# Linear attention and a PReLU feed-forward on one core: block 2's attention in rows with one column tile, and batches 0 and 1 used as loaded

## The chip, the cores and the metric

The kernel runs on one core of a Trainium2 chip. The metric is device time in microseconds. The core's engines each run their own queue of instructions: TensorE (PE in the profile; PEld are its weight loads), VectorE (DVE), ScalarE (ACT), GpSimd (POOL) and SyncE (SP). Here POOL issues the loads, SP issues the DMA transposes and some of the stores. Matmuls write PSUM banks, from which VectorE and ScalarE read.

## The reference

```python
def _attn_ref(q, k, v, g_norm):                       # 8 batches, 8 heads, S = 576, D = 64
    kv = np.einsum('bhsd,bhse->bhde', k, v)
    out = np.einsum('bhsd,bhde->bhse', q, kv)
    rms = np.sqrt(np.mean(out * out, axis=-1, keepdims=True) + 1e-06)
    return out / rms * g_norm
def _moe_ref(x, w_in, w_out, alpha):                  # 4608 tokens, 512 -> 2048 -> 512
    h = x @ w_in
    g = np.maximum(h, 0.0) + alpha * np.minimum(h, 0.0)
    return g @ w_out
x = attn_out.transpose(0, 2, 1, 3).reshape(4608, 512)
```

Inputs and output are float32. The kernel computes in 16 bits and accumulates in 32.

## The kernel before

**Blocks and units.** The 4608 tokens are cut into nine blocks of 512 (w = 0 to 8). A batch has 576 tokens, so a block's four tiles of 128 tokens come from one or two batches. For each block the 2048 hidden columns are made in 16 units of 128: four 128x512 matmuls into one PSUM bank (L507, `m1_mm`), ScalarE's negative part (L514) and VectorE's sum of the two (L518), which gives `gt`, the PReLU in 16 bits. VectorE's and ScalarE's reads free the bank; from block 2 on there are two such banks (h1, h2).

**The second product.** Block 0's is done plainly (L539, 64 matmuls of 512 columns). For blocks 1 to 8 it is done by seven products of half size, in Strassen's manner: sums of `gt` on VectorE (L623 to L629, `s_sum`), sums of the weights (`w_sum`), 112 matmuls of 256 columns per block (L688, `prod_mm`), and reads of the finished products into the four quarters of the output (`y_read`, which reads p1, u2, c11, u3, c22, c21, c12). The products of block w − 1 are laid into the units of block w, seven to a unit, in the order 1, 6, 2, 7, 5, 4, 3, into two banks that change places.

**Attention.** The attention of block w + 1 is also laid into the units of block w (`attention`), in one of two forms. A pair is two neighbouring heads.
- Column form (blocks 0, 1, 2): q is transposed on TensorE (L327, `transposes`), k^T v is made for a pair at a time (L371, `step_kv`) and masked to its two 64x64 diagonal squares by VectorE (L379); the output stands with head dimensions on the partitions (L393, `step_ot`), ScalarE squares it (L400), a matmul with a mask of ones sums the squares over the partitions (L416, `ssq_mm`), ScalarE takes the reciprocal root (L420), VectorE multiplies it and g in (L429, `norm`) and writes `xt`.
- Row form (blocks 3 to 8, `W_ROW = 3`): q is transposed by DMA on SP (`dma_t`); k^T v is made per head in 64x64 matmuls, one head of the pair to the left, one to the right half of the columns (L1001, `row_kv`; ScalarE copies them, L1007); the output stands with tokens on the partitions (L452, `rows_mm`, 64x64 matmuls); ScalarE squares 128x512 (L463, `rows_sq`), VectorE sums 64 at a time (L469, `rows_ssq`), ScalarE takes the root (L479), VectorE multiplies (L487, `rows_norm`), and a DMA transpose on SP brings the tile into `xt` (L492).

**Copies.** Batches are loaded by POOL into stages. Batch 0's q and k are regrouped by VectorE for heads side by side (L217, `regroup0`); batch 1's and batch 2's in large copies (`regroup`); from batch 3 on q is loaded ready for the DMA transpose, and ScalarE copies k pair by pair (L195, `regroup_pair`). g is multiplied into w_in by ScalarE during block 2 (`scale_w_in`), so that the norm of later blocks leaves it out.

**Order.** The order on PE, ACT, DVE, POOL and SP is that in which the code issues instructions; tables give the unit of each step (`ATT_1`, `ATT_AT`, `ROW_AT`, `S_AT`, `S_ROW`, `Y_READS`). Before the first unit, block 0's attention is worked out with TensorE kept warm by dummy matmuls (L295), and 64 matmuls of block 0's second product share its units with batch 1's attention.

Of the kernel before, what the change touches and what calls it, by code (L numbers as in the profile page):

```python
# [17 lines left out]
def kernel(  # L18
# [11 lines left out]
    nc = tc.nc  # L30
# [20 lines left out]
    W_ROW = 3  # L51
# [81 lines left out]

    alpha_row = ysb_p.tile([P, D_MODEL], FP32, name="y_sb")
# [11 lines left out]
    for i in range(NBUF):  # L146
        t = {}
        for nm in ("k", "v", "q") if i < 2 else ("k", "v"):
            n = 1 if nm == "v" else T0 if i == 0 else NT
            t[nm] = qkv_p.tile([P, n, H, D], FP16, name=f"{nm}sb{i}")  # L150
            if i > 0 or nm == "v":
                nc.vector.memset(t[nm][REM:P, n - 1, :, :], 0.0)
        bufs.append(t)
    stages = {}

    def load0(nm, j, n=1):
        i, h = divmod(2 * j, HH)
        if (0, nm, i) not in stages:
            stages[0, nm, i] = stage_p.tile([P, HH, T0, D], FP16, name=f"{nm}st", tag=f"{nm}st")
# [5 lines left out]
    def load_main(b, nm, h0=0, h1=H):  # L165
        if (b, nm) not in stages:
            stages[b, nm] = stage_p.tile([P, H, TPP, D], FP16, name=f"{nm}st", tag=f"{nm}st")
# [5 lines left out]
    def load_q(b):  # L173
        st = stage_p.tile([P, TPP, H, D], FP16, name="qst", tag="qst")
# [7 lines left out]
    def buf_of(b, nm):  # L182
        return bufs[min(b, B_NAT) % 2 if nm == "q" else b % NBUF][nm]

    def load_rem(b, nm):
        nc.gpsimd.dma_start(
            out=buf_of(b, nm)[0:REM, 0 if nm == "v" else TPP, :, :],
            in_=srcs[nm][b, :, MAIN:S, :].rearrange("h s d -> s h d"),
        )
# [13 lines left out]

    def load_gated(b):
        load_rem(b, "q")
        if b == B_NAT:
            load_q(b)
        load_rem(b, "k")
        load_main(b, "k")
        if b > B_NAT:  # L210
            load_q(b)
        load_rem(b, "v")
        load_main(b, "v")

    def regroup0(nm, j, n=1):
        i, h = divmod(2 * j, HH)
        nc.vector.tensor_copy(  # L217
            out=bufs[0][nm][0:P0, :, 2 * j : 2 * (j + n), :].rearrange("p t h d -> p h t d"),
            in_=stages[0, nm, i][0:P0, h : h + 2 * n],
        )  # L220

    def regroup_pair(b, nm, j):
        regroup(b, nm, 2 * j, 2 * j + 2, nc.scalar)

# [17 lines left out]
    def scale_w_in(g):  # L242
        i = max(n for n, f0 in enumerate(IN_CUTS[:-1]) if f0 <= g * P)
        f0 = g * P - IN_CUTS[i]
        blk = w_in_sb[i][:, :, f0 : f0 + P]
        nc.scalar.activation(out=blk, in_=blk, func=AF.Copy, scale=g2col[:])

    def load_w_out(i):
        t = w_p.tile([P, GW, D_MODEL], FP16, name=f"w_out_sb{i}")
        for r in range(0, GW, GW // 2):  # L250
            g = i * GW + r
            nc.gpsimd.dma_start(
                out=t[:, r : r + GW // 2, :],
                in_=moe_w_out[g * P : (g + GW // 2) * P, :].rearrange("(g p) m -> p g m", p=P),
            )
        w_out_sb.append(t)
# [20 lines left out]
    for i in range(len(IN_CUTS) - 1):  # L277
        load_w_in(i)
    load_batch(1, ("k",))
    load_w_out(0)  # L280
    load_main(1, "q")
    load_w_out(1)
# [3 lines left out]
    load_w_out(2)  # L286
    load_w_out(3)
    load_rem(1, "q")

# [13 lines left out]
    kv_masked = [const_p.tile([P, NPAIR, P], FP16, name=f"kv_masked{i}") for i in range(2)]  # L303
# [19 lines left out]

    def transposes(qt_ps, c, b, j, ts):
        n = rows(b)
        for t in ts:
# [29 lines left out]
    def dma_t(b, ts=tuple(range(NT))):  # L356
        qt = qt_sb[b % 2][:, :, PAD : PAD + S]
        for t in ts:
            c0, c1 = t * P, min((t + 1) * P, S)
            src = stages[b, "q"][:, t] if t < TPP else buf_of(b, "q")[0:REM, TPP]  # L360
# [5 lines left out]

    def step_kv(b, j, pool=(ps_s, "s")):
        ks, vs = pair_cols(b, "k", j), pair_cols(b, "v", j)
        kv_ps = pool[0].tile([P, P], FP32, name="kv_ps", tag=pool[1])
        for t in range(n_runs(b)):  # L370
            nc.tensor.matmul(  # L371
                out=kv_ps[:],
                lhsT=ks(t),
                rhs=vs(t),
                start=(t == 0),
                stop=(t == n_runs(b) - 1),
            )
        kvs[b, j] = kv_masked[b % 2][:, j, :]
        nc.vector.tensor_mul(out=kvs[b, j], in0=kv_ps[:], in1=mask32[:])  # L379

# [3 lines left out]
    def step_ot(w, j, pool=None, parts=1):  # L384
# [13 lines left out]
        sq = attn_p.tile([P, W], FP16, name="sq_sb")  # L398
# [27 lines left out]
    def norm(w, j, parts=1):  # L426
        ot_ps, rstd = ots.pop((w, j))
        for c in col_parts(parts):
            nc.vector.scalar_tensor_tensor(  # L429
# [9 lines left out]
    def rows_mm(w, i0):  # L439
        o_ps = row_tile([2, 2, NPAIR, D], "or_ps")  # L440
        for i in (i0 + 1, i0):
            b, r = divmod(w * W + i * P, S)
            for j in range(NPAIR):
# [5 lines left out]
                for n, (bb, c) in enumerate(steps):  # L449
                    for h in range(2):  # L450
                        part = slice(h * D, (h + 1) * D)
                        nc.tensor.matmul(  # L452
                            out=o_ps[:, h, i - i0, j, :],
# [4 lines left out]
            ots[w, "r", i] = o_ps[:, :, i - i0]  # L458

    def rows_sq(w, i):  # L460
        o_ps = ots.pop((w, "r", i))
        sq = attn_p.tile([P, 2, NPAIR, D], FP16, name="sq_sb")
        nc.scalar.activation(out=sq[:], in_=o_ps, func=AF.Square)  # L463
        ots[w, "r", i] = (o_ps, sq)

    def rows_ssq(w, i):
        o_ps, sq = ots.pop((w, "r", i))
        ssq = attn_p.tile([P, 2, NPAIR], FP32, name="ssq_r")
        nc.vector.tensor_reduce(  # L469
            out=ssq[:].rearrange("p h j -> p (h j)"),  # L470
            in_=sq[:].rearrange("p h j d -> p (h j) d"),
            axis=mybir.AxisListType.X, op=ALU.add,
        )
        ots[w, "r", i] = (o_ps, ssq)

    def rows_rs(w, i):
        o_ps, ssq = ots.pop((w, "r", i))
        rstd = attn_p.tile([P, 2, NPAIR], FP32, name="rstd_r")
# [5 lines left out]
    def rows_norm(w, i):  # L484
        o_ps, rstd = ots.pop((w, "r", i))
        xr = attn_p.tile([P, NPAIR, 2, D], FP16, name="x_rows", tag="rstd" if i % 2 else "x_rows")
# [9 lines left out]
    gts = {}  # L496
# [15 lines left out]
    def m1_evac(h_ps, w, g):  # L512
        m_sb = gt_p.tile([P, W], FP32, name="m_sb", bufs=2)
        nc.scalar.activation(out=m_sb[:], in_=h_ps[:], func=AF.Relu, scale=-1.0)  # L514
        i, r = divmod(g, 2)
        if (w, i) not in gts:
            gts[w, i] = gt_p.tile([P, 2, W], FP16, name="gt", tag=f"gt{i}")
        nc.vector.scalar_tensor_tensor(  # L518
            out=gts[w, i][:, r, :], in0=m_sb[:], scalar=beta_sb[:, g : g + 1], in1=h_ps[:],
            op0=ALU.mult, op1=ALU.add,  # L520
        )

# [14 lines left out]

    def y_mm(y, w, a, g):
        nc.tensor.matmul(  # L539
            out=y[:], lhsT=gt_cols(w, g, a * P, (a + 1) * P), rhs=w_out_blk(g),  # L540
            start=(g == 0), stop=(g == NF - 1),
# [3 lines left out]
    store_turn = [0]  # L545

# [28 lines left out]
    def y_out(y, w, a):  # L575
        y_sb = ysb_p.tile([P, D_MODEL], FP32, name="y_sb")
        nc.scalar.copy(out=y_sb[:], in_=y[:])
        store_rows(w * W + a * P, y_sb[:], 0, D_MODEL)
# [37 lines left out]
    def s_sum(w, n, k):  # L616
        lo, hi = gts[w, k], gts[w, k + KQ]
        a11, a21 = lo[:, :, 0:HW], lo[:, :, HW:W]
        a12, a22 = hi[:, :, 0:HW], hi[:, :, HW:W]
        t = sum_p.tile([P, 2, HW], FP16, name=f"s{n}", tag=f"s{n}{k}", bufs=2 if n < 3 else 1)  # L620
# [13 lines left out]
    def y_bank(w, n, a):  # L634
        pool, tag = ((ps_y, "y"), (ps_h, "h0"))[(w + (n != "Y")) % 2]
# [108 lines left out]
    Y_ORDER = (1, 6, 2, 7, 5, 4, 3)  # L744
    Y_LIST = [(n, i) for n in Y_ORDER for i in range(2 * NK)]
    PER = len(Y_LIST) // NF
    Y_READS = {2: ("p1",), 5: ("u2",), 7: ("c11",), 9: ("u3",), 11: ("c22",), 14: ("c21",)}
    R_ROW = {2: ("p1",), 5: ("u2",), 7: ("c11",), 14: ("c21",)}
    R_FIRST = {10: "u3", 12: "c22"}
    G_ORDER = [0, 1, 8, 9, 2, 3, 10, 11, 4, 5, 12, 13, 6, 7, 14, 15]  # L750


# [36 lines left out]
    regroup0("q", 1)  # L789
    keep_warm(1)  # L790
    step_t(0, 1, h_at(1))
    regroup0("k", 1)
# [5 lines left out]
    regroup0("q", 2, 2)  # L798
    keep_warm(1)
    step_t(0, 2, h_at(0))  # L800
    regroup0("k", 2)
# [6 lines left out]
    regroup0("k", 3)  # L808
# [358 lines left out]
```

## Time and profile before

| what | value |
|---|---|
| time, median of three runs | 274.64 us (274.28 to 275.09) |
| profiled execution, its own time | 275.59 us |
| its span, first to last instruction | 273.6 us |
| mean granted TensorE clock | 0.994 |
| first unit of block 0 / of block 1 / last matmul's end | 16.05 / 48.09 / 270.27 us |
| DMA | 34.56 MB, mean 126 GB/s |

The span is what the profiler recorded; 2.0 us of the execution's time lie around it. On the page, busy shares are averages over the whole span; the forty slices are 6.8 us each. In a group's line the first figures are an engine's busy time and the mean duration of one; matmuls are pipelined, so that a duration is longer than the distance from one start to the next. What stands in brackets behind an instruction is how long its engine was idle before it, and what released it.

### The profile page before, as it was taken

How to read it: one execution, taken by the hardware profiler on the slowest of the kernel's cores; microseconds unless marked ns; L12 is line 12 of the kernel's file. 1: busy time of each engine (PE TensorE's matmuls, PEld its weight loads, DVE VectorE, ACT ScalarE, POOL GpSimd, SP SyncE). 2: the span in 40 equal slices, each digit the busy share in tenths (PEclk: the TensorE clock that was granted, in tenths of full speed). 3: DMA queues.
4: the chain of work that ended last, by engine and by line, in shares of the span. 5: the costliest groups of instructions: out<-in, count | busy, mean ns of one | idle time of the engine just before them, and what ended most of it. 6: DMA issues, size and time to landing. Idle time of an engine off the chain costs nothing.

```text
span 273.6 us, 5687 instructions
## 1 busy us (share of the span) xinstructions
PE 266.3 (97%) x2181; PEld 170.8 (62%) x2181; DVE 227.9 (83%) x432; ACT 155.9 (57%) x294; POOL 86.2 (32%) x123
## 2 busy tenths in 40 slices
PE   7799999999999999999999999999999999999995
PEld 2364464555666766666666666666666666666794
DVE  6459938899889979997999799979998999877863
ACT  3267555879989865645565556555544553443210
POOL 8773462780733355226421551100110012000200
PEclk9799999999999999999999999999999999999999
DMA  8999999999999689966996699720222122201223
GB/s 161 196 200 199 197 202 189 220 112 162 137 164 180 99 129 149 170 153 113 155 167 147 112 156 164 151 89 19 77 60 77 22 77 60 77 1 41 77 79 116
DMA packets 87343, 34.56 MB, mean 126 GB/s; under 512 B 58884, under 2 KB 85652, under 8 KB 87316
## 3 DMA queue, kind: packets, MB, share of 16 engines
q0 software_dynamic: 58064, 24.35, 69.5%
q1 hardware_dynamic: 28212, 8.83, 17.1%
q10 hardware_dynamic: 1040, 1.02, 1.2%
q8 instruction: 17, 0.28, 0.4%
q14 instruction: 10, 0.08, 0.1%
HBM read 36.71 MB, written 9.44 MB: 169 GB/s over the span
## 4 chain that ended last, share of the span: by engine, by line
PE 95%; DMA 2%; DVE 1%; issue 0%; ACT 0%; POOLq 0%
PE h_ps L507 43%; PE yY L688 15%; PE yX L688 10%; PE yZ L688 10%; PE y L539 5%; DMA vst<-in_v_dram 2%; PE h_ps L530 2%; PE kv_ps L371 2%; PE or_ps L452 1%; PE kv_ps L1001 1%; PE ssq_ps L416 1%; PE qt_ps L327 1%; PE ot_ps L393 1%; PE yZ L683 1%; PE warm_ps L295 0%
## 5 line engine op out<-in xcount | busy, mean ns | idle before, releaser
L507 PE MATMUL h_ps<-xt,w_in_sb 128*128 128x512 f16 x544 | 136.9, 379 | 0.0
L514 ACT ACTIVATE m_sb<-h_ps 128x512 f32<-128x512 f32 x144 | 86.1, 599 | 78.1 <-PE h_ps L507 67.7
L518 DVE SCALAR_TENSOR_TENSOR gt<-m_sb,beta_sb,h_ps 128x512 f16<-128x512 f32 x144 | 106.2, 744 | 24.1 <-ACT m_sb L514 22.5
L507 PEld LDWEIGHTS <-w_in_sb 128*128 128x128 f16 x544 | 52.1, 98 | 40.0
L550 POOL DMA_DIRECT2D out_dram<-y_sb x36 | 22.6, 630 | 134.3 <-ACT y_sb L726 53.4
L688 PEld LDWEIGHTS <-s 128*128 128x128 f16 x496 | 48.5, 98 | 19.1
L688 PEld LDWEIGHTS <-gt 128*128 128x128 f16 x384 | 37.3, 98 | 14.0
L688 PE MATMUL yY<-wsum,s 128*128 128x256 f16 x256 | 36.3, 273 | 0.0
L688 PE MATMUL yX<-w_out_sb,gt 128*128 128x256 f16 x256 | 36.1, 273 | 0.0
L177 POOL DMA_DIRECT2D qst<-in_q_dram x20 | 17.7, 923 | 1.8 <-DMA vst<-in_v_dram 1.8
L688 PE MATMUL yY<-wsum,gt 128*128 128x256 f16 x128 | 17.6, 273 | 0.0
L688 PE MATMUL yZ<-wsum,s 128*128 128x256 f16 x120 | 16.7, 273 | 0.0
L688 PE MATMUL yZ<-w_out_sb,s 128*128 128x256 f16 x120 | 16.7, 273 | 0.0
L487 DVE TENSOR_TENSOR x_rows<-or_ps,rstd_r 128x512 f16<-128x512 f32 x24 | 16.4, 683 | 0.0
L469 DVE TENSOR_REDUCE ssq_r<-sq_sb 128x8 f32<-128x512 f16 x24 | 16.3, 678 | 0.0
L463 ACT ACTIVATE sq_sb<-or_ps 128x512 f16<-128x512 f32 x24 | 14.4, 599 | 2.6 <-PE or_ps L452 2.6
L539 PE MATMUL y<-w_out_sb,gt 128*128 128x512 f16 x64 | 15.8, 379 | 0.0
L625 DVE TENSOR_TENSOR s<-s,gt 128x512 f16<-128x512 f16 x32 | 13.5, 421 | 0.5
L623 DVE TENSOR_TENSOR s<-gt 128x512 f16<-128x512 f16 x32 | 13.4, 418 | 0.0
L629 DVE TENSOR_TENSOR s<-gt,s 128x512 f16<-128x512 f16 x32 | 13.2, 417 | 0.0
L627 DVE TENSOR_TENSOR s<-gt 128x512 f16<-128x512 f16 x32 | 13.0, 418 | 0.0
L720 DVE TENSOR_TENSOR u<-yY,p 128x512 f32<-128x512 f32 x16 | 10.9, 683 | 1.9 <-PE yY L688 1.7
(88 smaller groups left out, 249.9 us busy)
## 6 DMA issues: line engine op xcount, KB each, us to landing
out_dram<-y_sb POOLq DMA_DIRECT2D x16, 256.0 KB, 2.7
kst<-in_k_dram POOLq DMA_DIRECT2D x7, 512.0 KB, 7.9
vst<-in_v_dram POOLq DMA_DIRECT2D x6, 512.0 KB, 10.5
qst<-in_q_dram POOLq DMA_DIRECT2D x20, 128.0 KB, 8.0
w_out_sb<-in_moe_w_out_dram POOLq DMA_DIRECT2D x8, 256.0 KB, 11.7
out_dram<-y_sb SPq DMA_DIRECT2D x5, 256.0 KB, 2.2
w_in_sb<-in_moe_w_in_dram POOLq DMA_DIRECT2D x2, 512.0 KB, 10.0
qst<-in_q_dram POOLq DMA_DIRECT2D x2, 512.0 KB, 12.1
```

The lines of the kernel that those rows point to most:

```text
L177: nc.gpsimd.dma_start(out=st[:, t, :, :], in_=srcs["q"][b, :, t * P : (t + 1) * P, :].rearrange("h p d -> p h d"),)
L463: nc.scalar.activation(out=sq[:], in_=o_ps, func=AF.Square)
L469: nc.vector.tensor_reduce(out=ssq[:].rearrange("p h j -> p (h j)"), in_=sq[:].rearrange("p h j d -> p (h j) d"), axis=mybir.AxisListType.X ...
L487: nc.vector.tensor_tensor(out=xr[:].rearrange("p j h d -> p h j d"), in0=o_ps, in1=rstd[:].unsqueeze(3).to_broadcast([P, 2, NPAIR, D]), op ...
L507: nc.tensor.matmul(out=h_ps[:], lhsT=w_in_blk(c, g), rhs=xts[w][:, c, :], start=(c == 0), stop=(c == NC - 1),)
L514: nc.scalar.activation(out=m_sb[:], in_=h_ps[:], func=AF.Relu, scale=-1.0)
L518: nc.vector.scalar_tensor_tensor(out=gts[w, i][:, r, :], in0=m_sb[:], scalar=beta_sb[:, g : g + 1], in1=h_ps[:], op0=ALU.mult, op1=ALU.add,)
L539: nc.tensor.matmul(out=y[:], lhsT=gt_cols(w, g, a * P, (a + 1) * P), rhs=w_out_blk(g), start=(g == 0), stop=(g == NF - 1),)
L550: engs[store_turn[0] % len(engs)].dma_start(out=dst, in_=src)
L623: nc.vector.tensor_add(out=t[:], in0=a21, in1=a22)
L625: nc.vector.tensor_sub(out=t[:], in0=sums[w, 1, k][:], in1=a11)
L688: nc.tensor.matmul(out=bank, lhsT=lhs, rhs=rhs, start=fresh, stop=(c == NK - 1), skip_group_check=True,)
```

## The change

What the changed kernel does otherwise:

1. `W_ROW` is 2: block 2 takes the row form, except its tile 3, which is done in columns with all four pairs in one bank (`cols_mm`, `cols_sq`, `cols_rs`, `cols_norm`). Batch 2's q is transposed by DMA.
2. Batches 0 and 1 are read from their stages as loaded. Their key-value products are done per head, one head in each half of the columns, and their q transposes too. `regroup0`, `regroup(1, ...)` and `regroup_pair` go; the row form's key-value products read k and v of later batches from the stages (`head_rows`).
3. In the row form the square and its sum over 64 are one ScalarE instruction per head and tile, with an accumulator, unless the table's `red` is 1 for that tile (block 2's three row tiles, one tile of blocks 4 to 7, two of block 8), where they stay one square of 128x512 and a VectorE reduce.
4. w_in is scaled by g during block 0 and the first four units of block 1, mostly on VectorE; from block 1 on the norm leaves g out.
5. Products 1 and 2 of block w are laid into block w's own units and the first two of the next block (`x_prods`, bank y); the other five of block w − 1 go into the units of block w in the order 6, 7, 4, 5, 3 (`yz_prods`, bank h0). Where a read of a product falls in a unit, the unit's `gt` is made after it. The units go in plain order 0 to 15, and the sums have new tables.
6. Loads are issued in another order, those of batches from 3 on unit by unit, some behind a one-element POOL copy of a `gt` (`gate`); three stores of block 0 move to SP in block 2.

```diff
-    W_ROW = 3
+    W_ROW = 2
+    def head_rows(b, nm, h, t):
+        if t < TPP:
+            return stages[b, nm][:, h, t, :]
+        return rem_of(b, nm)[:, h, :]
     def transposes(qt_ps, c, b, j, ts):
+            for i in range(2):
+                src = cols0("q", j, i, t) if b == 0 else head_rows(b, "q", 2 * j + i, t)
+                nc.tensor.matmul(
+                    out=qt_ps[i * D : (i + 1) * D, c : c + n], lhsT=src,
+                    rhs=ident16[0:n, 0:n], is_transpose=True, start=True, stop=True,
...
     def step_kv(b, j, pool=(ps_s, "s")):
+        kv_ps = pool[0].tile([P, D], FP32, name="kv_ps", tag=pool[1])
+        for t in range(NT):
+            for i in range(2):
+                nc.tensor.matmul(
+                    out=kv_ps[i * D : (i + 1) * D, :], lhsT=head_rows(b, "k", 2 * j + i, t),
+                    rhs=head_rows(b, "v", 2 * j + i, t), start=(t == 0), stop=(t == NT - 1),
...
+    def cols_mm(w, i):
+        t = row_tile([2, NPAIR, P], "oc_ps")
+        for j in range(NPAIR):
+            nc.tensor.matmul(
+                out=t[:, 0, j, :], lhsT=kvs[b, j], rhs=qts[b, j][:, r : r + P],
...
     def rows_sq(w, i, half):
+        if ROW_AT[w]["red"][i]:
+            if half == 0:
+                nc.scalar.activation(out=sq[:], in_=o_ps, func=AF.Square)
+            else:
+                nc.vector.tensor_reduce(...)
+            return
+        for j in range(NPAIR):
+            nc.scalar.activation(
+                out=sq[:, half, j], in_=o_ps[:, half, j], func=AF.Square,
+                accum_out=ssq[:, half, j : j + 1],
+            )
...
-    regroup0("k", 3)
...
+    X_LIST, YZ_LIST = products(1, 2), products(6, 7, 4, 5, 3)
+    X_AT = [0, 0, 1, 3, 1, 0, 2, 3, 2, 3, 1, 0, 3, 0, 2, 7, 1, 3]
+    YZ_AT = [3, 6, 7, 5, 5, 6, 7, 3, 6, 8, 4, 4, 6, 5, 5, 0]
...
+    ROW_AT = {2: {'kv': 5, 'mm': {0: ((0,),), 7: ((1, 2), (3,))}, 'sq': (1, 1, 7, 7, 7, 8, 8, 9),
+        'rs': (3, 8, 9, 12), 'norm': (5, 9, 11, 13), 'red': (1, 1, 1, 1)}, 3: {'kv': 2, 'mm': {4:
+        ((1, 0), (3, 2))}, 'sq': (4, 4, 5, 6, 8, 8, 7, 9), 'rs': (6, 7, 9, 11), 'norm': (6, 7, 10,
+        11), 'red': (0, 0, 0, 0)}, 8: {'kv': 99, 'mm': {1: ((1, 0), (3, 2))}, 'sq': (1, 1, 3, 4, 6,
+        6, 9, 9), 'rs': (5, 5, 8, 12), 'norm': (6, 7, 9, 12), 'red': (0, 0, 1, 1)}}
+    for w in range(4, B):
+        ROW_AT[w] = {'kv': 3, 'mm': {4: ((1, 0), (3, 2))}, 'sq': (5, 5, 4, 6, 7, 7, 7, 8), 'rs': (6,
+            7, 8, 11), 'norm': (6, 9, 8, 11), 'red': (0, 0, 1, 0)}
+    COL_TILES = ((2, 3),)
...
+            behind = w > 1 and bool(yz_reads(w - 1, u))
...
+                m1_mm(h_ps, w, u, range(NC))
+                m1_neg(h_ps, w, u)
+                if not behind:
+                    m1_sum(h_ps, w, u)
...
+            x_prods(w, u)
+            if w > 1:
+                yz_prods(w - 1, u)
+            if behind:
+                m1_sum(h_ps, w, u)
```

## The prediction

> **What bounds the kernel now.** I read the page from the top: busy shares, the forty slices, the chain of work that ended last.
>
> ```profile
> PE 266.3 (97%) x2181; PEld 170.8 (62%) x2181; DVE 227.9 (83%) x432; ACT 155.9 (57%) x294; POOL 86.2 (32%) x123
> ...
> PE   7799999999999999999999999999999999999995
> ...
> PE 95%; DMA 2%; DVE 1%; issue 0%; ACT 0%; POOLq 0%
> ```
>
> TensorE is full in all slices but the first two and the last, and it is 95% of the chain. So two things move the end: instructions that leave or join TensorE's stream, and waits. To price the stream I read TensorE's timeline in a stretch that holds the row form, by starts and not by durations (matmuls overlap):
>
> ```profile
> 70.01 1.03 PE L507 MATMUL h_ps<-xt,w_in_sb 128*128 128x512 f16 x4
> ...
> 71.73 0.32 PE L1001 MATMUL kv_ps<-vst,ksb 128*64 128x64 f16 x8
> 71.88 0.20 PE L1001 MATMUL kv_ps<-vsb,ksb 128*64 128x64 f16 x2
> ...
> 72.36 0.20 PE L1001 MATMUL kv_ps<-vsb,ksb 128*64 128x64 f16 x2
> 72.49 1.04 PE L507 MATMUL h_ps<-xt,w_in_sb 128*128 128x512 f16 x4
> 73.36 0.93 PE L688 MATMUL yY<-wsum,s 128*128 128x256 f16 x7
> 74.22 0.76 PE L452 MATMUL or_ps<-kv_masked,qt_sb 64*128 64x64 f16 x40
> ```
>
> Four 128x512 matmuls and seven of 256 columns fill 72.49 to 74.22; over the trace start to start is 0.216 us for 512 columns, 0.163 for 384, 0.109 for 256, 0.056 for 128 and 0.043 for 96. Forty 64x64 key-value matmuls take 71.73 to 72.49, 0.76 us: two column halves start together, so they cost 16 ns each and about 0.1 us at the change of form on either side. The attention matmuls in rows (L452) cost 17.5 ns each with those changes, 14.9 without.
>
> The other place is the start, before the first unit of the first product (16.05 us):
>
> ```profile
> 15.09 0.35 DVE L217 COPY ksb<-kst 96x768 f16<-96x768 f16 x1
> 15.35 0.74 DVE L429 SCALAR_TENSOR_TENSOR xt<-ot_ps,g2col,rstd 128x512 f16<-128x512 f32 x1
> 15.49 0.51 PE L371 MATMUL kv_ps<-vst,ksb 96*128 96x128 f16 x6 [0.30 <-DVE ksb L217]
> 16.05 0.60 PE L815 MATMUL h_ps<-xt,w_in_sb 128*128 128x256 f16 x4
> ```
>
> Here TensorE waits for VectorE's regroup copies. Last, the two evacuating engines, in a steady window (columns: PE, weight loads, DVE, ACT, POOL, clock, DMA share, GB/s) and by shape:
>
> ```profile
> 130.00:160.00 30.00, 30.00 (x270) 20.08 (x269) 27.16 (x50) 17.75 (x36) 12.88 (x18) 1.00 1.15 146
> ```
> ```profile
> L463 ACT ACTIVATE sq_sb<-or_ps 128x512 f16<-128x512 f32 x24 | 14.4, 599 | 2.6 <-PE or_ps L452 2.6
> L469 DVE TENSOR_REDUCE ssq_r<-sq_sb 128x8 f32<-128x512 f16 x24 | 16.3, 678 | 0.0
> L1007 ACT CAST kv_masked<-kv_ps 64x256 f16<-64x256 f32 x10 | 3.7, 368 | 2.0 <-PE kv_ps L1001 2.0
> ```
> ```profile
> 16.97 0.66 ACT L400 ACTIVATE sq_sb<-ot_ps 128x256 f16<-128x256 f32 x2
> ```
>
> TensorE is never idle there, VectorE is busy 27.2 of 30 us, ScalarE 17.8.
>
> **The sum's base.** All durations are of one execution: 275.59 us, of which 273.6 is the span and 2.0 lies around it. It is 0.95 above the median of the runs, 274.64; I subtract the savings from the median.
>
> **TensorE's stream after the start.**
> (a) Batch 2's 20 transposes of 128 columns become DMA transposes: 20 × 0.056 = −1.12.
> (b) Batch 2's 20 key-value pair matmuls (1.12) become 40 halves with their change of form (0.76 + 0.1 = 0.85): −0.27.
> (c) Block 2's attention: four of 128 plus four of 384 columns (0.87) and four sums of squares of 512 (0.86) leave, 1.74; for three tiles come 24 matmuls × 14.9 ns (0.36) with two changes of form (0.38), and for the column tile four of 128 and one of 512 (0.44): 1.18. −0.56.
> (d) Batch 1's 20 pair matmuls (1.12) become 40 halves at 16 ns (0.64), in three groups with 0.19 of changes each (0.57): +0.09.
> (e) Batch 1's 16 full transposes (0.90) become 32 of 64 columns wide. If halves run side by side, as the key-value halves do, they add only two changes, +0.38. If not, 16 × 0.056 = 0.90 on top. The nearest row is the 40 halves in 0.76 us: I take +0.38.
> Block 0's halves lie in the start, below. All other matmuls keep number and shape: moving the products to other units moves nothing in the sum. Sum −1.48 (−0.58 if (e) goes badly).
>
> A rule that speaks against (b), (d) and (e): the Trainium skill, page "TensorEngine Tiling (Array Packing)", Restrictions, says that column tiling disables the fast weight load. In the trace the weight loads of the halves are 112 ns against 98 for full ones, yet 40 matmuls with them fit into 0.76 us, so they are hidden behind each other; were (e)'s loads laid end to end they would be 32 × 112 ns = 3.6 us in place of 0.9 and the total +2.7 worse. The trace speaks against that for key-value halves and does not show transposes.
>
> **The start.** Of the copies of L217, five leave VectorE (0.35 to 0.79 each), and keys, values and q of block 0 go to TensorE as loaded. The last copy held TensorE 0.30 (line above) and the two before it held earlier transposes and key-value groups; between them they sit on the chain to 16.05, behind values that land at about 8.0 us and cannot come earlier. Upper bound of the gain: 1.0, lower 0 if ScalarE's rstd (0.69, ended 15.14) and the norm (0.74) set the end anyway. I take −0.75, since the queue that this norm stood in loses two copies. The chunks then pair 96x96 transposes in 64-column halves: 48 instead of 24, side by side.
>
> **VectorE and ScalarE.** VectorE loses 15 reduces (678 ns), four of the regroup copies of 2048 columns (0.68 to 0.78), five of L217 and four masks; it gains eight scalings of w_in (about 0.7 each, laid in block 0 and block 1's first units, where it has 6.14 of 8 us busy). It ends lighter by some 11 us (16.7 less, 5.6 more), which costs nothing and gains nothing while TensorE is full. ScalarE loses 18 copies of k (611 ns) and 15 squares of 599, and gains 144 squares of 128x64 with a row sum in the accumulator. No row shows an accumulator. From the squares of 256 columns (two in 0.66 us, 0.28 start to start; 0.83 ns per column): 64 columns without accumulator start every 0.12 us. If the accumulator is written as by one more small instruction (the 128x8 row, 298 less 100 of overlap), 0.32. I take 0.22, midway, as neither row is nearer; the cover is TensorE's own stretch. In units 4 to 8 of a steady block TensorE needs five units of 0.864, 35 products of 0.109 and the 24 attention matmuls with changes (0.79): 8.9 us. ScalarE needs five negations (0.49 start to start), one big square and three rstd (0.2): 3.56 + 24x. That equals TensorE's at x = 0.22, and two h banks and four row tiles lend about 0.9: nothing is lost below x = 0.26.
>
> The Trainium skill, "ScalarE: Activation LUTs", section "What ACT_TABLE_LOAD costs", gives 186 ns plus 0.833 per column, with about 93 overlapped: an estimate of 0.146 for 64 columns against 0.12 from the rows, which would leave 0.11 instead of 0.14 for the accumulator and does not change the sign.
>
> **What the moved queues cost.** In block 1, batch 2 now needs its values at unit 5 (about 54.1) for the row key-value products; they landed at 53.7 and POOL's issues before it change (the same loads in another order; six stores that held POOL 3.1 us behind it go to SP later). Its q chunks are transposed on SP from unit 0 on (landing 2.4 to 5.8 after issue, 48.8 and later) and are needed at unit 7 (57.4): 57.2 at the latest. Both are met by under 0.4 us, and what waits is TensorE itself, with all of block 1 behind: I charge +0.5 (0 to +2). The delayed sums of units 2, 5, 8, 11, 14 stand behind a read of a product bank (0.76 + 0.3 + 0.68 + 0.74 = 2.48 against the 2.39 that two banks allow), and eleven gates on POOL hold loads behind a gt: +0.3 (0 to +1). The tail's order changes but its last products and final additions do not: 0.
>
> Total: −1.48 − 0.75 + 0.5 + 0.3 = −1.43, so 273.2.
>
> **Rivals.**
> 1. The accumulating squares are dear (slower). Above 0.26 us each, the four squares of a half stand before the next unit's negation, the h bank comes free late, and TensorE waits in units 4 to 8: 24 × (x − 0.26) in each of blocks 3 to 6, 32 in block 2's units. At x = 0.32 that is some 8 us: 281; at 0.40, 18 us. The row 298 ns for a tiny ScalarE instruction speaks for it, its 0.28 pair spacing for 256 columns against. Chance 0.20.
> 2. Batch 2 comes late (slower). With values or the last chunk 2 to 4 us behind 54.1 and 57.4, TensorE stops in block 1 for as long: 275.3 to 277.5. It decides once transposes land 0.4 later than now; the 0.2 of slack speaks for it, the stores moved out of its way against. Chance 0.13.
> 3. The halves of the transposes don't pair, or the start is bound by rstd and norm as before: (e) costs +0.9, or the start gives 0. 274.0 to 275.2, no change; chance 0.13. Were the weight loads of all 32 transposes laid end to end as well (32 × 112 ns, 2.7 more than taken), 275.9, slower: 0.02, as the forty halves in 0.76 us speak against it. The Trainium skill's rule on column tiling, cited at (e), would come to that.
> 4. As forecast, 271.6 to 273.8: chance 0.52.
>
> **How the numbers follow.** The time is that of case 4, 273.2. A measurement of this kernel tells about 0.3%, 0.82 us, from no change, so faster begins below 273.8. Faster: case 4, 0.52. Same: case 3 and the mild end of 2, 0.15. Slower: rest, 0.33. The range runs from 271.6 (full start gain, no waits) to 279, which leaves out the upper half of case 1 and a little at the bottom; case 4's own range is 271.6 to 273.8.
>
> **What would show it.** Right: TensorE's start to start unchanged per form; qt_ps transposes in halves paired a few ns apart; first 256-column L815 matmul near 15.3; steady ScalarE squares of 128x64 starting every 0.22 or less; block 1 with no wait of TensorE for vst or qt_sb. Wrong: TensorE idle in blocks 2 to 6 behind a negation that stands behind squares; kv_ps waiting for a DMA near 54; block time above the present 27.6.

## The result, and the profile after

The change makes the kernel slower by 0.6%: the ratio to the kernel before is 1.0058, 95% interval 1.0035 to 1.0081, about 276.0 us where the kernel before takes 274.45 (median of 21 runs, 274.09 to 275.62). The ratio leaves out nine of the changed kernel's 21 runs (274.25 to 282.62 us, median 277.74), those from 278.82 on, eight of which had a mean granted clock of 0.994 or 0.988, as one of 129 runs of the kernel before had in the later comparisons, so 0.6% is the low end of what the change costs. 273.2 was forecast. The profiled execution took 276.86 us, its span is 274.7.

The page of the changed kernel, busy shares, slices of TensorE and its clock, and the chain that ended last:

```profile
PE 265.0 (96%) x2286; PEld 168.0 (61%) x2286; DVE 216.9 (79%) x413; ACT 156.3 (57%) x532; POOL 86.0 (31%) x130
...
PE   7999999999999979999999999999999999999995
...
PEclk9999999999999999999999999999999999999999
...
PE 69%; DMA 19%; ACT 4%; DVE 3%; issue 2%; POOL 1%; DVEq 0%; POOLq 0%; ACTq 0%
```

TensorE was 95% of the chain and is 69% now; transfers went from 2% to 19%. TensorE's busy time fell from 266.3 to 265.0, and yet the span grew. TensorE's waits name the places (what waited, for what: us in all, times, longest):

```profile
PE h_ps L631 <- DMA xt<-x_rows: 2.4, 3, 1.8
...
PE y L643 <- DMA w_out_sb<-in_moe_w_out_dram: 0.6, 2, 0.4
PE oc_ps L512 <- DMA qt_sb<-qsb: 0.6, 1, 0.6
PE kv_ps L418 <- DVE kv_masked L393: 0.5, 1, 0.5
PE kv_ps L1122 <- DMA vst<-in_v_dram: 0.4, 1, 0.4
```

Those of the list that lie behind the first unit wait for a transfer, all but one (`kv_masked`, for VectorE). To split the difference I added up TensorE's start-to-start times, from the first matmul of the first unit on, and counted as a gap whatever a matmul took over 0.14 us longer than its columns need:

| us | before | after |
|---|---|---|
| start to the first unit's first matmul | 16.05 | 13.34 |
| from there to the last matmul's end | 254.21 | 258.34 |
| of it gaps | 0.6 | 6.3 |
| of it the stream | 253.6 | 252.0 |
| last matmul's end to the end of the span | 3.3 | 3.0 |

The stream is 1.6 us shorter, where 1.48 was forecast. Four of the gaps of after hold a change of form of about 0.1 us besides the wait, which the table counts as gap, so the stream's own saving is nearer 1.2. The gaps are 5.7 us longer (4.6 in a second profile of the same kernel), where 0.8 was forecast. The start is 2.7 us shorter, but most of that is not the change's: in the profile of before TensorE's granted clock was 0.5 for 3.4 us of the start (the 7 in its second slice), in this one it was not, and the first of batch 0's values, issued at 1.3 us in both, landed at 8.0 us before and at 6.5 after.

The largest wait is that of block 3's first unit for the last of its four row tiles. TensorE's timeline of after, with POOL's and then SP's beside it:

```profile
97.20 0.49 PE L796 MATMUL yY<-wsum,s 128*128 128x256 f16 x3
99.46 0.38 PE L631 MATMUL h_ps<-xt,w_in_sb 128*128 128x128 f16 x4 [1.77 <-DMA xt<-x_rows]
```
```profile
92.43 0.70 POOL L198 DMA_DIRECT2D vsb<-in_v_dram  x1
93.12 0.92 POOL L176 DMA_DIRECT2D vst<-in_v_dram  x1
```
```profile
92.11 1.20 SPq L585 DMA_TRANSPOSE xt<-x_rows  x1
93.40 1.78 SPq L380 DMA_TRANSPOSE qt_sb<-qsb  x1
```

The tile's transpose is issued at 92.11, beside a load of 512 KB of values that the gate now lets go in unit 11. It took 7.3 us to land. In the kernel before, the transpose in the same place was issued at 91.90 and landed in 2.5; there the values had been loaded from 76.57 on. The two landings, after (with the transpose issued at 90.3, which took 3.7) and before:

```profile
DMA to landing us min/median/max: 3.7/5.5/7.3
```
```profile
DMA to landing us min/median/max: 2.5/2.5/2.5
```

### The profile page after: what moved, and what is told of

The parts are those of the page before. It is cut to its first block, busy times and chain, and to the rows that moved or that the text cites. A ratio compares the mean times of both kernels' runs of the same rounds, so it can differ in the third digit from the quotient of the medians.

```text
span 274.7 us, 6154 instructions
## 1 busy us (share of the span) xinstructions
PE 265.0 (96%) x2286; PEld 168.0 (61%) x2286; DVE 216.9 (79%) x413; ACT 156.3 (57%) x532; POOL 86.0 (31%) x130
## 4 chain that ended last, share of the span: by engine, by line
PE 69%; DMA 19%; ACT 4%; DVE 3%; issue 2%; POOL 1%; DVEq 0%; POOLq 0%; ACTq 0%
PE h_ps L600 30%; PE yY L796 14%; PE yZ L796 8%; PE yX L796 8%; DMA w_out_sb<-in_moe_w_out_dram 5%; DMA xt<-x_rows 4%; PE y L643 4%; DMA w_in_sb<-in_moe_w_in_dram 3%; DMA vst<-in_v_dram 3%; ACT sq_sb L562 3%; DMA qst<-in_q_dram 2%; DMA qt_sb<-qsb 2%; PE h_ps L631 2%; PE kv_ps L1122 1%; PE or_ps L499 1%
## 5 line engine op out<-in xcount | busy, mean ns | idle before, releaser
L609 ACT ACTIVATE m_sb<-h_ps 128x512 f32<-128x512 f32 x144 | 88.3, 614 | 81.5 <-PE h_ps L600 59.0
L600 PEld LDWEIGHTS <-w_in_sb 128*128 128x128 f16 x540 | 51.3, 98 | 39.6 <-DMA w_in_sb<-in_moe_w_in_dram 0.4
L655 POOL DMA_DIRECT2D out_dram<-y_sb x32 | 20.5, 646 | 140.4 <-DVE y_sb L838 62.4
L796 PE MATMUL yX<-w_out_sb,gt 128*128 128x256 f16 x256 | 43.1, 273 | 0.0
L796 PE MATMUL yY<-wsum,s 128*128 128x256 f16 x256 | 35.2, 273 | 0.0
L562 ACT ACTIVATE sq_sb<-or_ps 128x64 f16<-128x64 f32 x144 | 31.7, 285 | 2.6 <-PE or_ps L499 2.6
L562 ACT ACTIVATION_READ_ACCUMULATOR sq_sb<-or_ps 128x1 f32 x144 | 31.2, 272 | 0.0
L580 DVE TENSOR_TENSOR x_rows<-or_ps,rstd_r 128x512 f16<-128x512 f32 x27 | 18.5, 687 | 0.9 <-ACT rstd_r L572 0.3
L731 DVE TENSOR_TENSOR s<-gt 128x512 f16<-128x512 f16 x32 | 12.9, 421 | 0.2
L735 DVE TENSOR_TENSOR s<-gt 128x512 f16<-128x512 f16 x32 | 12.4, 419 | 0.0
```

What stands on the lines that cost most here:

```text
L562: nc.scalar.activation(out=sq[:, half, j], in_=o_ps[:, half, j], func=AF.Square, accum_out=ssq[:, half, j : j + 1],)
L580: nc.vector.tensor_tensor(out=xr[:].rearrange("p j h d -> p h j d"), in0=o_ps, in1=rstd[:].unsqueeze(3).to_broadcast([P, 2, NPAIR, D]), op ...
L600: nc.tensor.matmul(out=h_ps[:], lhsT=w_in_blk(c, g), rhs=xts[w][:, c, :], start=(c == 0), stop=(c == NC - 1),)
L609: nc.scalar.activation(out=neg[w, g][:], in_=h_ps[:], func=AF.Relu, scale=-1.0)
L655: engs[store_turn[0] % len(engs)].dma_start(out=dst, in_=src)
L731: nc.vector.tensor_add(out=t[:], in0=a21, in1=a22)
```

## Experiments

Times are ratios to the kernel before on the same chip, with 95% intervals. Theory A: TensorE waits for transfers that land late because others share the DMA engines. Theory B: ScalarE's squares with accumulator, or the engines' own order, hold things up.

**The changed kernel again.** No edit.

> The changed kernel once more, as the yardstick on this chip and for its second profile. Theory A (TensorE waits for transfers that land late): the waits for vst, qt_sb, x_rows and w_out_sb come back at the same four places, with other sizes, since landings vary: 3 to 6 us of waits between 25 and 100 us, time 275 to 278. Theory B (ScalarE's squares with accumulator hold things up): the same waits with the same sizes, within 0.2 us, since engines' durations do not vary.

Measured 1.0091 (1.0074 to 1.0107). The waits came back in the same places, but for that for w_out_sb, which is too short for the list here, and with other sizes:

```profile
PE h_ps L631 <- DMA xt<-x_rows: 1.5, 3, 1.1
...
PE kv_ps L1122 <- DMA vst<-in_v_dram: 0.9, 1, 0.9
PE kv_ps L403 <- DMA vst<-in_v_dram: 0.7, 2, 0.4
PE oc_ps L512 <- DMA qt_sb<-qsb: 0.7, 1, 0.7
PE kv_ps L418 <- DVE kv_masked L393: 0.5, 1, 0.5
```

The wait for VectorE repeats (0.5 both times); those for transfers do not (1.8 to 1.1, 0.4 to 0.9).

**No accumulator.** Every tile with one square of 128x512 and a reduce:

```diff
-'red': (0, 0, 0, 0)}, 8: {... 'red': (0, 0, 1, 1)}
+'red': (1, 1, 1, 1)}, 8: {... 'red': (1, 1, 1, 1)}
-'norm': (6, 9, 8, 11), 'red': (0, 0, 1, 0)}
+'norm': (6, 9, 8, 11), 'red': (1, 1, 1, 1)}
```

> One change to the changed kernel: every row tile's squares are one square of 128x512 on ScalarE and a reduce on VectorE, as in the kernel before (no accumulator). Theory A: the waits of 25 to 100 us stay, steady blocks keep their time of 27.6 us; within 1 us of the changed kernel. Theory B: the wait for x_rows near 97 us goes and the time falls by 1.5 to 2 us.

Measured 1.0125 (1.0092 to 1.0159): not faster. The last x_rows transpose of block 3 was issued 78.4 us after the first unit, against 78.5 in the run above, so the squares had not delayed it; it landed in 4.7 us instead of 6.4, and that wait was absent in this profile. Later blocks got gaps of 0.16 and 0.29 us each that the changed kernel does not have. Theory B falls for the squares with accumulator; the engines' order is tested further down. The absent wait alone would have fitted both theories; the time of issue tells them apart.

**Values early.** The loads of values of batches 3 to 7 are issued five and eight units earlier.

```diff
-        q, k, v = (1, 5, 12) if w == 1 else (2, 1, 11)
+        q, k, v = (1, 5, 7) if w == 1 else (2, 1, 3)
```

> One change to the changed kernel: values of batches 4 to 7 are loaded from unit 3 of the block (was 11), those of batch 3 from unit 7 of block 1 (was 12). Theory A: the last x_rows transpose before block 3 (7.3 us to landing, issued at 92.1 just ahead of 512 KB of values) lands in 3 to 5 us, TensorE's 1.8 us wait for it goes, and so does the 0.4 us wait for vst at 73.7: 2 us faster than the changed kernel, 0.4% or more below the kernel before or level with it. Theory B: the x_rows transposes are issued late by ScalarE and the wait stays; time as the changed kernel.

Measured 1.0135 (1.0104 to 1.0165): slower, a miss. The two waits named did go, and another came:

```profile
PE yZ L796 <- DVE y_sb L840: 2.1, 1, 2.1
...
PE oc_ps L512 <- DMA qt_sb<-qsb: 1.1, 1, 1.1
```

The chain at that place runs through the stores of block 0 that SP issues at 85 us:

```profile
85.60 6.64 DMA out_dram<-y_sb
```

They landed after 6.6 us, beside the values (issued at 80.81), and held the y_sb buffer that VectorE needed to read out a product.

**The start alone.** In the kernel before, block 0's keys, values and q used as loaded (the changed kernel's key-value and transpose functions for batch 0):

```diff
-    regroup0("q", 1)
...
-    regroup0("k", 1)
...
-    regroup0("q", 2, 2)
...
-    regroup0("k", 2)
...
-    regroup0("k", 3)
```

> The kernel before with one part of the change: batch 0's keys, values and q used as loaded, in column halves, no regroup copies. By the prediction's step the first unit begins 0.75 us earlier. If the changed kernel's start (13.3 against 16.1 us) is this part's doing, 1.5 to 2.7 us earlier, and as the loads of w_out and batch 1 do not come earlier, part of that is given back in waits for them before 48 us: theory A says 0.5 to 1.5 us net faster than the kernel before (273.0 to 274.0); the rival that the start's gain is wholly given back says no change.

Measured 1.0009 (0.9999 to 1.0019): no gain. The first unit begins at 14.26 us instead of 16.05, of which 0.70 is this part's doing (worked out further down); the rest is an earlier landing of batch 0's values, 7.4 us, and the full clock. TensorE's timeline shows where it is given back:

```profile
30.67 1.89 PE L572 MATMUL y<-w_out_sb,gt 128*128 128x512 f16 x8
33.12 1.07 PE L341 MATMUL qt_ps<-ident,qsb 128*128 128x128 f16 x16 [0.56 <-DVE qsb L197]
```

TensorE arrives early at work whose input is not there: a gap of 0.72 us for batch 1's regrouped q. All gaps together are 0.87 us longer than in the kernel before, enough to take up the 0.70. The rival (gain wholly given back) holds.

**Half the loads.** Of the keys and values of batches 3 to 7 only heads 0 to 3 are loaded, and the products read these twice:

```diff
-            return stages[b, nm][:, h, t, :]
+            return stages[b, nm][:, h % HH if b >= 3 and nm != "q" else h, t, :]
...
-                    load_main(x[0], what)
+                    load_main(x[0], what, 0, HH)
```

> The changed kernel with half of the keys and values of batches 3 to 7 loaded (heads 0 to 3, which then stand for heads 4 to 7 too: that part of the computation is wrong, the instructions of the engines are the same). Theory A (the waits are for transfers that share the DMA engines): the wait for vst near 73.8 us and that for x_rows near 99 us go, 2 us or more faster than the changed kernel, near 274.5. Rival B (the waits come from the engines' own order): they stay, no change.

Measured 1.0037 (1.0016 to 1.0059), where the changed kernel lost 0.6% and 0.9% in its two comparisons; the gain is smaller than expected. The wait for vst at 73.7 went, the largest for x_rows fell to 0.6 us:

```profile
PE h_ps L631 <- DMA xt<-x_rows: 1.3, 3, 0.6
```

The order of every engine is the same, so for these two waits theory A holds: it is what is moved beside them. The time alone would not tell, since the interval overlaps that of the first comparison.

**Block 0's stores early, on POOL.**

```diff
-    LOADS.setdefault((2, 6), [])[0:0] = (("put", 0), ("put", 2), ("put", 1))
+    LOADS.setdefault((1, 10), [])[0:0] = (("put", 0), ("put", 2), ("put", 1))
...
-                    store_engines[0] = (nc.sync,)
+                    store_engines[0] = (nc.gpsimd,)
```

> One change to the changed kernel: the three output tiles of block 0 are stored by POOL in unit 10 of block 1, not by SP in unit 6 of block 2. Theory A: the y_sb buffers that they hold come free 20 us earlier and block 2 has 0.77 MB less to move; x_rows land 1 to 3 us earlier near 99 us and that wait (1.1 to 1.8) goes or shrinks, the wait for vst near 73.8 stays (0.4 to 0.9) since the values are still loaded late: 1 to 2 us faster than the changed kernel. If only the late values make the wait near 99, it stays.

Measured 1.0063 (1.0040 to 1.0085), between the two comparisons of the changed kernel, where 1 to 2 us less was expected. The wait near 99 us was gone, and unlike expected the one for vst too; the runs spread only from 275.21 to 278.07. With the values early as well, both edits together:

> Both moves: values loaded early and block 0's stores in unit 10 of block 1. Loading the values early alone made TensorE wait 2.1 us at 93 for a y_sb buffer whose store was caught behind those values. Theory A: with the stores out of the way neither that wait nor those for vst and x_rows of block 3 remain, so 3 to 4 us less than early values alone, 274 to 275: level with the kernel before. If it is slower than 276 the stores are not what held the buffer.

Measured 1.0144 (1.0107 to 1.0182), a miss again: batch 3's values, now loaded in unit 7 of block 1 (issued at 58.96, landed at 69.70), met the transposes of block 2's row tiles, the last of which landed at 72.79 after 7.7 us, and TensorE stood 4.4 us:

```profile
PE h_ps L631 <- DMA xt<-x_rows: 4.6, 2, 4.4
```

A fourth version moved the column tile and two banks besides:

```diff
-'mm': {0: ((0,),), 7: ((1, 2), (3,))}
+'mm': {0: ((0,),), 7: ((1, 2),), 8: ((3,),)}
...
-    step_kv(1, 2)
+    step_kv(1, 2, Q_POOL)
...
-    step_kv(1, 3, Q_POOL)
+    step_kv(1, 3, S_POOL)
```

> Both moves, and two more: block 2's column tile one unit later (its q chunk then is in place: the wait of 0.6 to 1.1 us at 57 goes), and the banks of batch 1's third and fourth key-value products exchanged (the 0.45 us wait for kv_masked at 38.3 goes). Theory A, every wait a transfer or a bank that came late: 1 to 1.5 us below both moves alone, 272.8 to 274, faster than the kernel before by 0.2 to 0.6%. If the time does not fall, the waits move on to the next late transfer.

Measured 1.0183 (1.0148 to 1.0219): the wait for qt_sb went, that for x_rows in the same place was 5.9 us. (Both profiles are of the longest of their version's runs, 281.0 and 285.0 us.) In these versions, what a move saves in one place it pays in another, while the same stretch has to carry the bytes.

**Keeping the values late, and removing one wait after another.** First block 2's column tile one unit later, by the `mm` line of the last diff, on top of the stores in unit 10:

> The changed kernel with block 0's stores in unit 10 of block 1, as before, and block 2's column tile one unit later. Theory A: the wait for qt_sb at 57 (0.6 to 1.1 us in all profiles so far) goes; 0.5 to 1 us faster than with the stores alone, ratio near 1.003. If the wait only moves to the x_rows transposes near 69 us, no change.

Measured 1.0077 (1.0047 to 1.0106): the wait at 57 went, but that for x_rows at 69 grew from 0.5 to 1.2 us. Then block 2's row tiles normed earlier and two memsets later:

```diff
-'norm': (5, 9, 11, 13), 'red': (1, 1, 1, 1)
+'norm': (5, 8, 9, 13), 'red': (1, 1, 1, 1)
...
-    for nm in ("k", "q"):
-        nc.vector.memset(bufs[0][nm][REM:P, TPP, :, :], 0.0)
     step_kv(1, 1, S_POOL)
...
     step_kv(1, 3, Q_POOL)
+    for nm in ("k", "q"):
+        nc.vector.memset(bufs[0][nm][REM:P, TPP, :, :], 0.0)
```

> As the last, and block 2's second and third row tiles are normed one and two units earlier (their DMA transposes begin 1 to 2 us earlier), and two memsets of VectorE come after batch 1's key-value masks. Theory A: the waits for xt near 69 us (0.2 to 0.5) and for kv_masked near 38.4 us (0.45) go too; what is left of the waits between 25 and 100 us is under 0.6 us, time 273 to 274.2, level with the kernel before or 0.3% faster.

Measured 1.0018 (1.0005 to 1.0030); the wait for VectorE (`kv_masked`), the one of the list that the engines' own order made, went with the memsets. The two transposes were issued 2.6 and 3.2 us earlier than with the stores alone (60.2 and 61.8 against 62.8 and 65.0), and landed at the same time: last at 68.6 against 68.9. First with the stores alone, then this version:

```profile
L585 SPq DMA_TRANSPOSE xt<-x_rows x2: 1194/1194/1195, 62.8 to 65.0; - x2
...
DMA to landing us min/median/max: 3.8/4.4/4.9
```
```profile
L585 SPq DMA_TRANSPOSE xt<-x_rows x2: 1383/1758/2134, 60.2 to 61.8; - x2
...
DMA to landing us min/median/max: 6.7/7.3/7.9
```

So the wait at 68.7 stayed (1.4 us). A w_out piece ahead of batch 1's keys:

```diff
-    load_main(1, "k")
     load_w_out(1)
+    load_main(1, "k")
```

> As the last, with the second piece of w_out loaded ahead of batch 1's keys. The wait of y for w_out_sb near 33 us (0.25 to 0.4) goes; if the loads before 40 us are one queue that is full, another wait in its place, for batch 1's keys or values, of the same size: no change.

Measured 1.0002 (0.9987 to 1.0018); the wait of y for w_out_sb was there as before, 0.4 us, so this profile, which is of the longest of its runs (276.23), shows no use of the exchange. To tell whether the late tiles wait for bytes, the stores were left out of the version before that, so that three tiles of the output are missing:

```diff
-                    store_rows(x[0] * P, late_out.pop(x[0])[:], 0, D_MODEL)
+                    late_out.pop(x[0])
```

> As the version with stores, column tile, norms and memsets moved, but the three stores of block 0 (0.77 MB, output rows 0 to 383) are left out. There the x_rows transposes near 61 us were issued 2.6 us earlier and landed no earlier. Theory A (the DMA engines are full from 48 to 70 us and the bytes ahead set the landing): without these bytes they land in 4 to 5 us instead of 6.7 to 7.9, the 1.4 us wait at 68.7 goes, time 1 to 1.5 us lower, ratio 0.997 to 0.999. Rival (the transposes wait for something of their own queue): the wait stays, no change.

Measured 1.0018 (0.9998 to 1.0039). The same two transposes, issued in the same instants:

```profile
L585 SPq DMA_TRANSPOSE xt<-x_rows x2: 1189/1190/1192, 60.2 to 61.8; - x2
...
DMA to landing us min/median/max: 4.2/4.5/4.9
```

For these two the bytes ahead were the cause, and not the order of the engines, which is otherwise the same. But batch 3's values were then 1.0 us late at 73.1, and the time did not fall. Values and stores exchanged; then the stores in unit 1 of block 2; then the later values earlier with that. The three settings of the two lines:

```diff
+        q, k, v = (1, 5, 10) if w == 1 else (2, 1, 11)
+    LOADS.setdefault((1, 14), [])[0:0] = (("put", 0), ("put", 2), ("put", 1))
...
+        q, k, v = (1, 5, 11) if w == 1 else (2, 1, 11)
+    LOADS.setdefault((2, 1), [])[0:0] = (("put", 0), ("put", 2), ("put", 1))
...
+        q, k, v = (1, 5, 11) if w == 1 else (2, 1, 7)
+    LOADS.setdefault((2, 1), [])[0:0] = (("put", 0), ("put", 2), ("put", 1))
```

> All moves so far, w_out piece ahead of batch 1's keys included, but block 0's stores only in unit 14 of block 1 and batch 3's values from unit 10 (was 12): 0.25 MB less ahead of the x_rows transposes of 60 to 62 us, and the stores fall where 63 GB/s were moved before. Theory A: the wait near 68.8 us falls from 1.4 to under 0.7 us, none for vst near 73; 273.5 to 274.2, ratio 0.996 to 1.000. If the wait keeps its size, bytes are not its cause.

> All moves, with block 0's stores in unit 1 of block 2 (from 70 us on, when 63 to 140 GB/s were moved) and batch 3's values from unit 11. In the version without these stores the x_rows transposes landed in 4.2 to 4.9 us, 1.4 us ahead of need, and the values 1.0 us late. Theory A (what lands last is set by the bytes ahead of it): x_rows wait near 69 under 0.4 us, vst wait near 73 under 0.5 us, ratio 0.995 to 0.999, faster than the kernel before. If the lost time only moves on (to k or q of batch 4, or a y_sb buffer held too long), no change against the kernel before.

> As the last, with the values of batches 4 to 7 loaded from unit 7 (was 11): they are off the DMA engines before block 3's last x_rows transposes at 92 us. Theory A: no wait for x_rows near 98 us, where the others have 0 to 1.9; 0 to 0.5 us faster than the last. If loads and stores then meet at 85 to 90 us, a wait of a product bank for y_sb comes in its place, as with early values alone.

Measured 1.0008 (0.9990 to 1.0026), 0.9994 (0.9976 to 1.0012) and 0.9995 (0.9975 to 1.0015). In the first, TensorE waited 1.7 us for x_rows: the values in place of the stores hold them up as much. In the second no x_rows were late, and the values were, by 1.7 us at 73.7; in the third by 1.3. The second's line:

```profile
PE kv_ps L1122 <- DMA vst<-in_v_dram: 1.7, 1, 1.7
```

So the last step keeps the second setting and moves the work that needs the values:

```diff
-3: {'kv': 2, 'mm': {4:
+3: {'kv': 3, 'mm': {4:
```

> As the version with block 0's stores in block 2, with batch 3's key-value products one unit later (3 instead of 2, as in the later blocks): they come at 74.8 us, and the values landed at 73.7. Theory A (order, not bytes): its one large wait, 1.7 us for vst at 73.7, goes, no wait between 40 and 230 us is over 0.5 us, and the time is 0.8 to 1.4 us lower: ratio 0.995 to 0.997, faster than the kernel before. If the wait comes back in another place, the bytes are the price and the change cannot win here.

Measured 0.9982 (0.9971 to 0.9994): 0.2% faster than the kernel before, 274.22 against 274.63 us, with an interval that just leaves out 1, and less than expected. Its page and TensorE's waits:

```profile
PE 265.7 (97%) x2286; PEld 168.1 (62%) x2286; DVE 216.6 (79%) x413; ACT 156.0 (57%) x532; POOL 89.3 (33%) x136
```
```profile
PE warm_ps L297 <- DVE y_sb L119: 1.5, 1, 1.5
PE kv_ps L403 <- DMA vst<-in_v_dram: 0.9, 1, 0.9
PE qt_ps L336 <- DVE qsb L898: 0.4, 1, 0.4
PE ssq_ps L460 <- ACT sq_sb L444: 0.2, 1, 0.2
```

All four lie before the first unit or at it; none is listed after 17 us. Gaps fell from 6.3 to 0.7 us with the same matmuls. This execution had the same 3.4 us at half the clock in its start as that of before, so the two can be compared: first unit 15.35 against 16.05, from there to the last matmul's end 253.45 against 254.21, tail 3.7 against 3.3.

## Why the prediction was wrong

**The stream (a) to (e): right in its mechanism, about 0.3 too large.** −1.48 was forecast. The changed kernel gives −1.6 by the table, −1.2 without the four changes of form that lie in its gaps. In the version without waits the stream is 0.85 shorter than before (the body 0.76), and it still holds three waits of about 0.1 us that are too short to count as gaps, which again makes about −1.2. Batch 1's key-value products took 1.00 us for 1.21, its transposes in halves paired as the key-value halves did: 24 of them and then 8, with a wait between, in TensorE's timeline of after:

```profile
32.04 0.86 PE L336 MATMUL qt_ps<-ident,qst 128*64 128x128 f16 x24
33.29 0.38 PE L643 MATMUL y<-w_out_sb,gt 128*128 128x512 f16 x1 [0.39 <-DMA w_out_sb<-in_moe_w_out_dram]
33.60 0.41 PE L336 MATMUL qt_ps<-ident,qst 128*64 128x128 f16 x8
33.94 0.39 PE L643 MATMUL y<-w_out_sb,gt 128*128 128x512 f16 x1
```

The eight, with two changes of form, hold TensorE from 33.60 to 33.94. Laid end to end at their mean of 109 ns, the eight weight loads alone would fill 0.9 us. So what the Trainium skill says in "TensorEngine Tiling (Array Packing)", Restrictions, that column tiling disables the fast weight load, costs nothing here that can be seen. The third rival falls in that half.

**The start: its size right at the first unit, wrong as a gain in the sum.** 0.75 was forecast, 0.70 came between the kernel before and the version without waits (16.05 and 15.35), two executions with the same slow stretch in which batch 0's first values landed at the same 7.99 us. The step took that landing as fixed at 8.0. Over the runs it lies between 6.5 and 8.4, and the first unit begins 6.8 to 7.1 us behind it at the full clock and 7.36 in the version without waits; by these figures, of the 2.7 us between the profiles of before and after, 1.5 are the landing, 0.5 the clock and 0.7 the change. The step also counted its gain in full, while the kernel before with this part alone was no faster: there the first unit came 1.8 us earlier, the loads of w_out and batch 1 that follow only 0.3 to 0.4. In this half the third rival held for the time, though not by the rstd and norm that it named.

**The squares: right.** 0.22 us each was taken, 0.20 measured; each is two instructions:

```profile
78.62 0.22 ACT L562 ACTIVATE sq_sb<-or_ps 128x64 f16<-128x64 f32 x1 [0.74 <-PE or_ps L499]
78.74 0.19 ACT L562 ACTIVATION_READ_ACCUMULATOR sq_sb<-or_ps 128x1 f32 x1
78.83 0.21 ACT L562 ACTIVATE sq_sb<-or_ps 128x64 f16<-128x64 f32 x1
```

The square starts the read 0.12 and the next square 0.21 us later; over eight of them 0.20. That is under the 0.26 at which the first rival would decide, and the list of TensorE's waits has none for a bank behind a negation. The first rival fell.

**What the moved queues cost: the step that failed.** It charged 0.5 for block 1 and 0.3 for the delayed sums and gates; the gaps came to 5.7 us more than before in one profile and 4.6 in the other. The second rival had the mechanism, a transfer of batch 2 that is late by more than its slack, and the wait for the q chunk at 57 (0.6 us) is that one. But it looked for it in one place. The step took landing times from the old profile as if they belonged to the transfers, and asked only when each would be issued. The changed kernel puts loads, stores and transposes of 48 to 100 us beside each other in a new order, and each then lands when the bytes around it have passed: 7.3 us for a transpose that took 2.5. The profile of before already had such landings one block later, where no one waited for them:

```profile
DMA to landing us min/median/max: 4.1/7.7/7.8
```

The gates and the stores put off to block 2 were priced by the queues that issue them, not by the transfers that they meet.

The rule behind it stands in the Trainium skill, "DMA: Bandwidth & Descriptors", section "Issuing engines are not separate DMA queues": transfers started by different engines run on the same 16 DMA engines and interleave. The runs agree: SP's transposes landed 2.8 us sooner (median 4.5 for 7.3) when POOL's 0.77 MB were left out, with nothing changed on SP.

What stays open: the version without waits is 1.1 us shorter than the kernel before in the two profiles, which had the same slow stretch in their start, but only 0.4 us in the medians. Of the 12 and 17 runs behind these medians only the profiled one shows a clock under 0.998, so the 0.4 is what is left without that stretch; why it costs the kernel before more (its profiled execution was 1.0 above its median, that of this version 0.1) was not tested. Nor was it separated which of the six parts of the change moved which transfer. Nor was the tail taken apart, which ran from 2.9 to 3.8 us over the versions of the changed kernel.

## What to carry to other kernels

When a kernel's main engine is full and its transfers land with some tenths of a microsecond to spare, a change to the order of loads or stores has to be priced at the landings: list what else is moved in the same stretch, and take the landing time from a row with as many bytes around it. Issuing late transposes earlier did not help here while the bytes ahead of them stayed; what helped was to take bytes out of the stretch, and to move the work that needs what lands late. Here a shorter instruction stream was worth nothing until the waits that came with it were gone, and they were found one behind the other.

## What the hardware showed that was not expected

A long enough wait of TensorE in the middle of the kernel cost more than itself. In the version with early values alone, TensorE stood still for 2.2 us before 93.1, and the granted clock then was 0.5 for 3.4 us (the windows' columns: PE, weight loads, DVE, ACT, POOL, clock, DMA share, GB/s):

```profile
90.00:93.60 3.60, 1.54 (x12) 0.94 (x11) 1.24 (x2) 0.60 (x1) 0.25 (x1) 1.00 1.34 294
93.60:97.00 3.40, 3.40 (x13) 1.55 (x12) 2.75 (x7) 0.60 (x1) 0.95 (x2) 0.50 0.86 155
97.00:100.00 3.00, 3.00 (x22) 2.01 (x21) 2.34 (x6) 1.03 (x2) 0.00 (x0) 0.99 0.47 92
```

A stall of 4.5 us was followed by 3.4 us at half the clock, one of 6.0 us by 6.8 us. Those of up to 1.9 us in the middle of the other profiles were followed by none. At half the clock 3.4 us do the work of 1.7, so by estimate this wait of 2.2 us cost 3.9. One such stretch lowers the mean granted clock over 275 us to 0.994, two lower it to 0.988. The Trainium skill, "TensorE: Matmul & The Clock Gate", section "What's actually happening", puts the drop after at least one idle window of about 3.4 us; here 2.2 us were enough in one case, and the length of the slow stretch agrees with that window.
